# Another searched order of the same jobs: a one-core transformer layer with windowed attention and a gated MLP

## Chip, core and metric

The kernel runs on one core of one Trainium2 chip. The metric is the device time of one launch in microseconds (us). Before the change the median of three runs is 244.9 us (244.74 to 245.12).

## What is computed

One layer on 2048 tokens of width 448: an attention part with 16 heads of 28, in which a query sees 8 keys at distances 0, 2, ... 14, and then a gated MLP (width 896 twice) whose gate mixes all tokens by a 2048 x 2048 matrix.

```python
def _A_ref(x, wqkv, wo):
    qkv = (x @ wqkv).reshape(B, S, 3, H, Dh).transpose(2, 0, 3, 1, 4)
    ...
    logits = jnp.einsum('bhsd,bhswd->bhsw', q, kg) * scale
    logits = jnp.where(mask[None, None, :, :], logits, -1000000000.0)
    o = jnp.einsum('bhsw,bhswd->bhsd', _softmax(logits), vg)
    return o.transpose(0, 2, 1, 3).reshape(B, S, D) @ wo

def _B_ref(x, w_in, w_sp, b_sp, w_out):
    z = _gelu(jnp.einsum('bsd,df->bsf', x, w_in))
    z1, z2 = z[..., :Fh], _layernorm(z[..., Fh:])
    g = jnp.einsum('ts,bsf->btf', w_sp, z2) + b_sp[None, :, None]
    return jnp.einsum('bsf,fd->bsd', z1 * g, w_out)
...
h = x + _A_ref(_layernorm(x), A_wqkv, A_wo)
h2 = h + _B_ref(_layernorm(h), B_w_in, B_w_sp, B_b_sp, B_w_out)
```

## The kernel before

The program is written as some 890 **jobs**. A job is a short run of instructions on one engine: PE (matmul), ACT, DVE, POOL, or SP, which issues the DMAs. The engines run their own lists, in the order in which the jobs stand in the table `ORDER`, and each instruction waits on semaphores for what it needs. Nothing is reordered when the kernel runs: an instruction that waits holds all that stands behind it on its engine. Further tables belong to that order: `BANKS` gives each matmul group its PSUM banks, `ON` puts a copy on another engine than its default, and `MODE` tells how a matmul product over 448 rows (three full chunks of 128 and a rest of 64) is split into two jobs a and b: FH (full chunks, then the rest), HF (rest first), or AB, in which each chunk is taken as two halves of 64 rows that run on the two halves of the array, so that a and b each do one half. Number 885 in `ORDER` is a small matmul without use, `warm` (L1077), that keeps PE busy while it has nothing to do.

The stages, as the names in this document have them (the lines are those of the profile):

- **Loads** (L519): x in five pieces and more, named by their first tile of 128 tokens (x0, x1, x2 with x3, x4 with x5, x6 with x7, x8 with three more, x12 with three more), the q,k weights wq in five pieces (wq0, wq1, wq2 of 128 rows, wq3 and wq4 of 64), wv and wo in three pieces each, w_in in eight.
- **Layernorm of x** by tile: statistics st (L620) and mv (L622) on DVE, the power of -1/2 on POOL (L611), the normalisation n (L631) into a ring xn, and a copy nd (L504) that doubles the last 64 columns, on POOL or DVE. Tiles 0 to 3 are transposed on PE (L661) and copied to xhT by xe; tiles 4 to 15 by a transposing DMA xT (L518).
- **q,k**: wp copies wq into a padded wqk (L504); qk0 and qk1 (128 tokens each, L704), qk2 (256), qk3, qk4, qk5 (512 each, L461, in four groups), copied to qkT by qe.
- **Attention** in 17 blocks b of up to 128 keys: the value product v (L461, two blocks at once), logits lg (L809, two halves), exponentials ex (ACT, L818), a mask multiplication mk on DVE (L824), the block product o (L833), the division (rc, om: L841, L844), a doubling copy od, a transposing DMA oT, and a copy oc that interleaves even and odd tokens.
- **Projection** y (two tiles at once, L461), the add h on DVE (L774), the second layernorm, and a transposing DMA hT of two tiles.
- **MLP**: z2 and z1 (L461) with gelu on ACT, statistics and normalisation of z2, the gate products g (L987, L1008) with w_sp, which is loaded by 32 transposing DMAs wlo and whi, the gate's add and multiplication on DVE (L968, L971), and the output product wo (L1035, L1056), add and store.

All DMAs are issued by SP, one after the other. A transposing DMA keeps SP for about 1.3 us:

```python
def dma_T(name, dst, src, reads, writes, key):
    return load(name, dst, src, writes, 1.27, (TLAT, 0.56), key=key, transpose=True, reads=reads)
```

What a product waits for follows from what it reads. The value product of blocks b and b + 1 reads the x tiles that these blocks cover, so v4 needs the tiles 3, 4 and 5; qk5 needs the tiles 12 to 15:

```python
product("v%d" % b, key, f, r_wv + xh_res(lo, hi), D, tk, [o_jobs.get(b + i - NV) for i in range(nb)])
```

The order is fixed by one function that reads the tables:

```python
def order(self):
    for t, b in zip(self.tickets, BANKS):
        t.b = b
    return [self.jobs[i] for i in ORDER]
```

Of the kernel before, what the change touches and what calls it, by code (L numbers as in the profile page):

```python
# [9 lines left out]
FH = 896  # L10
# [9 lines left out]
NPT = 4  # L20
TLAT = 0.67
MODE = {'qk2_0': 'AB', 'qk2_1': 'AB', 'qk2_2': 'AB', 'qk2_3': 'FH', 'qk3_0': 'AB', 'qk3_1': 'AB', 'qk3_2': 'AB',
# [8 lines left out]
ORDER = [6, 26, 42, 27, 43, 29, 0, 885, 30, 885, 1, 31, 885, 885, 7, 885, 885, 28, 12, 885, 32, 885, 2, 52, 885, 134,  # L31
# [40 lines left out]
BANKS = [2, 1, 2, 1, 6, 4, 2, 6, 4, 0, 4, 0, 4, 0, 6, 4, 0, 0, 2, 4, 4, 4, 2, 4, 6, 3, 6, 6, 6, 6, 0, 4, 6, 7, 2, 0,  # L72
# [4 lines left out]
KEY = dict(x=-10.145, xs=0.685, qk=-3.702, qkg=-1.064, v=-1.761, ve=-6.148, qe=-3.15, lg=-1.488, ex=5.497,  # L77
           mk=-3.215, o=2.696, om=0.603, oT=-1.054, hh=0.0, y=-5.759, h=0.564, ln2=4.478, hT=19.942, z2=74.834,
           z2s=0.028, zr=2.556, zrs=0.21, z1=34.42, z1s=2.041, g=84.462, gs=0.172, wo=1.509, wl=-9.273,
           wls=4.361, wp=-9.955)  # L80
WINB = 2
ON = {'xe3_0': 'dve', 'nd0_4': 'dve', 'nd0_5': 'dve', 'nd0_7': 'dve', 'nd0_8': 'dve', 'nd0_10': 'dve', 'nd0_13':
         'dve', 'nd0_14': 'dve', 'qe3_1': 'dve', 'qe4_1': 'dve', 'qe4_2': 'dve', 've0': 'dve', 'od0': 'dve', 'od2':
         'dve', 'oc2': 'act', 'oc3': 'act', 'od5': 'dve', 'oc5': 'dve', 'nd1_2': 'dve', 've6': 'dve', 'od6': 'dve',
         'oc6': 'act', 'od7': 'dve', 've8': 'dve', 'oc8': 'act', 'od9': 'dve', 'oc9': 'act', 'oc9b': 'act', 'nd1_6':
         'dve', 'oc10': 'dve', 'oc11': 'act', 'nd1_8': 'dve', 've12': 'dve', 'od12': 'dve', 'nd1_11': 'dve', 'oc14':
         'dve', 'nd1_12': 'dve', 'od16': 'dve', 'nd1_15': 'dve', 'z2c10': 'dve'}
RAW2 = [0, 1, 2, 1, 1, 1, 1, 2, 1, 2, 1, 0, 0, 1, 0, 0]
XEH = {0: 2}
WLH = [4, 4, 8, 9, 18, 1, 4, 12, 24, 4, 14, 34, 6, 22, 21, 26]  # L90
# [1044 lines left out]
```

## Time and profile before

| | |
|---|---|
| median of the runs | 244.9 us |
| the profiled execution's own time | 247.0 us |
| its span, first to last instruction | 245.3 us |
| mean granted TensorE clock | 0.993 |
| weight loads of PE | busy 122.3 us, beside the matmuls |
| shares of the chain that ended last | PE 80%, DMA 8%, DVE 7%, ACT 1% |
| median from issue to landing: x in pieces of 224 KB | 3.4 us |
| the same: wq in pieces of 224 KB | 4.5 us |
| the same: transposes OTs, hnT, wsp_hi | 2.9, 3.8, 4.2 us |

Sizes of the loads: x 112 KB a tile; wq 224 KB for each of the three large pieces and 56 KB for each of the two small ones; wv and wo 336 KB and twice 56 KB each. The chain that ended last is found from the end of the execution backwards: at each step what released an instruction, or the one before it on its engine. The engines' busy times overlap. The rows of the profile stand in the prediction, where they are used.

### The profile page before, as it was taken

Reading aid. Unit: us, or ns where it says so; the run is one execution under the profiler, and the core shown is the slowest. Engines: PE = TensorE matmul, PEld = TensorE weight load, DVE = VectorE, ACT = ScalarE, POOL = GpSimd, SP = SyncE. Lnnn points to the kernel's source line nnn. Section 1 sums busy time; section 2 is a strip of 40 time slices with the busy share of each in tenths; the row PEclk is TensorE's granted clock in tenths of the full one; section 3 lists DMA queues with packets and bytes.
Section 4 is the critical chain, followed back from the end, with each engine's and each line's share of the span. In section 5 each row is a group of like instructions: output and inputs, shape, how many; then the busy total and the mean of one; then the engine's idle time right before and its main releaser. Section 6 shows DMA issues by size and latency. Waiting matters only on the chain.

```text
span 245.3 us, 5632 instructions
## 1 busy us (share of the span) xinstructions
PE 237.2 (97%) x2422; PEld 122.3 (50%) x2422; DVE 147.6 (60%) x334; ACT 91.1 (37%) x109; POOL 42.5 (17%) x98
## 2 busy tenths in 40 slices
PE   7997999999999989999999999999999999999995
PEld 4763544554555534444555555555554444444453
DVE  5998685998999897899913030604217350060584
ACT  2485748968899956659711000000000000000000
POOL 6625022030533317052311000000000000000000
PEclk9997999999999999999999999999999999999999
DMA  6953527989688889957999700000000020000022
GB/s 175 294 157 70 129 61 110 189 174 186 128 107 112 88 146 225 253 59 134 166 178 181 141 3 0 3 0 3 0 3 0 0 92 24 0 3 0 3 90 97
DMA packets 66233, 23.20 MB, mean 95 GB/s; under 512 B 58656, under 2 KB 65952, under 8 KB 66208
## 3 DMA queue, kind: packets, MB, share of 16 engines
q1 hardware_dynamic: 66208, 22.83, 48.5%
q8 instruction: 19, 0.31, 0.5%
q14 instruction: 6, 0.05, 0.1%
HBM read 6.72 MB, written 1.84 MB: 35 GB/s over the span
## 4 chain that ended last, share of the span: by engine, by line
PE 80%; DMA 8%; DVE 7%; ACT 1%; SPq 1%; issue 1%; POOL 0%
PE psum L987 37%; PE psum L461 27%; PE psum L1035 7%; DMA hnT<-xn 4%; PE psum L1008 3%; PE psum L809 2%; PE psum L833 2%; PE psum L1056 2%; DMA wq<-in_A_wqkv_dram 2%; DVE st L620 2%; DMA xhT<-xn 2%; DVE E L824 1%; DVE xn L631 1%; DMA OTs<-otm 1%; DVE x_tm L774 1%; SPq L519 1%
## 5 line engine op out<-in xcount | busy, mean ns | idle before, releaser
L968 DVE TENSOR_TENSOR ub<-psum,bb 128x512 bf16<-128x512 f32 x28 | 18.1, 686 | 64.4 <-PE psum L987 64.4
L987 PE MATMUL psum<-wsp_hi,z2p 64*128 64x512 bf16 x384 | 42.2, 376 | 0.0
L818 ACT ACTIVATE E<-psum 128x960 bf16<-128x960 f32 (+2 forms) x34 | 31.5, 976 | 6.3 <-PE psum L809 6.3
L987 PEld LDWEIGHTS psum<-wsp_hi,z2p 64*128 64x128 bf16 x384 | 19.7, 94 | 21.9 <-DVE srg L1016 0.4
L987 PE MATMUL psum<-wsp_lb,z2p 64*128 64x512 bf16 x224 | 26.9, 376 | 0.0
L987 PE MATMUL psum<-wsp_la,z2p 64*128 64x512 bf16 x224 | 26.5, 376 | 0.0
L461 PE MATMUL psum<-w_in,hnT 64*128 64x448 bf16 (+1 forms) x206 | 24.6, 350 | 0.2 <-issue 0.2
L461 PE MATMUL psum<-hnT,w_in 64*128 64x512 bf16 (+1 forms) x166 | 23.7, 377 | 1.1 <-DMA hnT<-xn 0.9
L461 PE MATMUL psum<-xhT,wqk 64*128 64x512 bf16 (+3 forms) x206 | 24.4, 355 | 0.1
L898 DVE BATCH_NORM_STATS2 st<-z2p 128x6 f32<-128x448 bf16 x32 | 19.0, 610 | 8.0 <-ACT z2p L894 6.0
L824 DVE TENSOR_TENSOR E<-E,maskb 128x1920 bf16<-128x1920 bf16 (+2 forms) x17 | 19.8, 1183 | 2.9 <-ACT E L818 2.9
L620 DVE BATCH_NORM_STATS2 st<-x_tm 128x6 f32<-128x448 bf16 x32 | 18.8, 613 | 1.4 <-DMA x_tm<-in_A_x_dram 1.3
L987 PEld LDWEIGHTS psum<-wsp_lb,z2p 64*128 64x128 bf16 x224 | 12.8, 94 | 11.4
L987 PEld LDWEIGHTS psum<-wsp_la,z2p 64*128 64x128 bf16 x224 | 12.8, 94 | 11.4
L611 POOL TENSOR_TENSOR rs<-rs,negh 128x2 f32<-128x2 f32 (+2 forms) x23 | 17.4, 758 | 3.0 <-DVE rs L610 1.1
L936 ACT ACTIVATE z1p<-psum 128x1024 bf16<-128x1024 f32 x14 | 14.1, 1023 | 10.0 <-PE psum L461 10.0
L1035 PE MATMUL psum<-w_out,z1p 128*128 128x448 bf16 x84 | 16.4, 353 | 0.0
L461 PEld LDWEIGHTS psum<-w_in,hnT 64*128 64x128 bf16 (+1 forms) x206 | 10.9, 94 | 10.8 <-issue 1.0
L461 PE MATMUL psum<-wv,xhT 64*128 64x448 bf16 (+1 forms) x92 | 14.9, 367 | 1.4 <-DMA xhT<-xn 1.4
L504 ACT ACTIVATE qkT<-psum 128x1024 bf16<-128x1024 f32 (+1 forms) x17 | 13.3, 824 | 6.9 <-PE psum L461 4.2
L461 PEld LDWEIGHTS psum<-hnT,w_in 64*128 64x128 bf16 (+1 forms) x166 | 9.6, 95 | 12.4 <-DVE x_tm L774 1.4
L461 PEld LDWEIGHTS psum<-xhT,wqk 64*128 64x128 bf16 (+1 forms) x206 | 10.0, 95 | 9.8 <-issue 0.8
(68 smaller groups left out, 254.6 us busy)
## 6 DMA issues: line engine op xcount, KB each, us to landing
w_in<-in_B_w_in_dram SPq DMA_DIRECT2D x8, 224.0 KB, 3.7
out_dram<-srg SPq DMA_DIRECT2D x16, 112.0 KB, 1.7
x_tm<-in_A_x_dram SPq DMA_DIRECT2D x2, 448.0 KB, 5.2
w_out<-in_B_w_out_dram SPq DMA_DIRECT2D x1, 784.0 KB, 5.1
wq<-in_A_wqkv_dram SPq DMA_DIRECT2D x3, 224.0 KB, 4.5
x_tm<-in_A_x_dram SPq DMA_DIRECT2D x3, 224.0 KB, 3.4
bb<-in_B_b_sp_dram SPq DMA_DIRECT2D x1, 512.0 KB, 4.8
wv<-in_A_wqkv_dram SPq DMA_DIRECT2D x1, 336.0 KB, 4.8
```

What stands on the lines that cost most here:

```text
L461: ins = e.matmul(o, w, x, start=k not in seen, stop=last, **kw)
L504: j = pl.job(name, eng, key, [(lambda e: e.activation(o(), i(), AF.Copy) if eng == "act" else e.tensor_copy(o(), i()), list(reads), list(w ...
L611: power = (lambda e: e.tensor_tensor(R, A, negh[:, 0:1].to_broadcast([128, n]), ALU.pow), [rr, r_negh], r_rs[k][m:m + n])
L620: [(lambda e: e.bn_stats(st[:, m, :], src), [rsrc], [r_st[k][m]])], dve_t(D))
L818: return e.activation(o, i, AF.Exp, scale=SCALE)
L824: return e.tensor_tensor(a, a, maskb[:, mi:mi + 1, pad:pad + nq].to_broadcast([NK, NHEAD, nq]), ALU.mult)
L898: [(lambda e, m=m, k=k: e.bn_stats(st3[:, m, k, :], z2p[:, m, D * k:D * (k + 1)]), [r_z2[m]], [r_st[2][m]])], dve_t(D))
L936: return e.activation(o, i, AF.Gelu_apprx_tanh)
L968: [(lambda e: e.tensor_tensor(ub[:, s, :], psv(tk, k), bb[:, 512 * tc:512 * tc + 512], ALU.add), [r_bb], [r_ub[s]])], dve_t(512), use=[tk] ...
L987: ins = e.matmul(psv(tk, k), z2p[h, s, 128 * fc:128 * fc + 128], wsp(s, tc)[h], start=n == 0 and s == 0, stop=n == len(lots) - 1 and s == ...
L1008: ins = e.matmul(psv(tk), z2p[:, s, 128 * fc:128 * fc + 128], wsp(s, tc), start=(s == 0), stop=(s == NB - 1))
L1035: ins = e.matmul(psv(tk, k, D), z1p[h, fc, 128 * (m + k):128 * (m + k) + 128], w_out[h, fc, :], start=fc == 0 and (which == 0 or not half) ...
```

## The change

The jobs are the same but for the number of `warm` matmuls and for the splits in `MODE`; their order (`ORDER`), banks (`BANKS`), engines (`ON`) and splits are another solution of the same search. The tables' first differing rows:

```diff
-ORDER = [6, 26, 42, 27, 43, 29, 0, 885, 30, 885, 1, 31, 885, 885, 7, 885, 885, 28, 12, 885, 32, 885, 2, 52, 885, 134,
...
+ORDER = [6, 29, 33, 26, 134, 0, 34, 7, 885, 27, 885, 1, 885, 885, 31, 2, 885, 885, 885, 52, 11, 885, 42, 885, 32, 3,
...
-ON = {'xe3_0': 'dve', 'nd0_4': 'dve', 'nd0_5': 'dve', 'nd0_7': 'dve', 'nd0_8': 'dve', 'nd0_10': 'dve', 'nd0_13':
...
+ON = {'xe0_1': 'act', 'xe1_0': 'dve', 'xe2_0': 'dve', 'xe3_0': 'dve', 'nd0_6': 'dve', 'nd0_8': 'dve', 'nd0_10': 'dve',
+         'nd0_12': 'dve', 'nd0_13': 'dve', 'nd0_14': 'dve', 'nd0_15': 'dve', 'wp1': 'act', 'wp2': 'act', 'qe2_3':
...
```

The file is one line longer, so each line of the program stands one lower.

In `MODE` 16 products had FH or HF before and 15 have it now. In `ON` the weight copies wp1 and wp2 and the second half of x's tile 0 go from DVE to ACT, the evacuations of tiles 1 and 2 from ACT to DVE, nd0_4 and nd0_5 from DVE to POOL; of the q,k copies DVE has five and not three, of the V copies two and not four, of the z2 copies two and not one.

**SP's queue at the start.** The names x_tm, wq and wo are the loads of x, of the q,k weights and of the output weights; a form 128x448 is one tile of x, 128x2x448 two. Before (the third row is x2 and x6, the last one x4):

```order
L519 DMA x_tm<-in_A_x_dram 128x448 x2
L519 DMA wq<-in_A_wqkv_dram 128x896
L519 DMA x_tm<-in_A_x_dram 128x2x448 x2
L519 DMA wq<-in_A_wqkv_dram 128x896
L519 DMA wq<-in_A_wqkv_dram 64x448
L519 DMA wq<-in_A_wqkv_dram 128x896
L519 DMA wq<-in_A_wqkv_dram 64x448
L519 DMA wo<-in_A_wo_dram 64x448
L519 DMA wv<-in_A_wqkv_dram 64x448
L519 DMA x_tm<-in_A_x_dram 128x2x448
```

Now (the pairs of tiles are x2, x4 and x6, in this order):

```order
L520 DMA x_tm<-in_A_x_dram 128x448 x2
L520 DMA x_tm<-in_A_x_dram 128x2x448
L520 DMA wq<-in_A_wqkv_dram 128x896 x2
L520 DMA x_tm<-in_A_x_dram 128x2x448
L520 DMA wq<-in_A_wqkv_dram 128x896
L520 DMA wo<-in_A_wo_dram 128x3x448
L520 DMA wq<-in_A_wqkv_dram 64x448 x2
L520 DMA x_tm<-in_A_x_dram 128x2x448
```

x2 and x4 moved ahead; x6 moved back, behind the last pieces of wq, which themselves stand behind the large piece of wo.

**PE around the first product that needs a tile transposed by DMA (v4).** The names V and E are the values and the exponentials, qkT holds q and k; the first 448 wide rows are v0 before and v2 now, the last row is v4. Before:

```order
L461 MATMUL psum<-wv,xhT 128x448 [waits sem_pe]
L461 MATMUL psum<-wv,xhT 128x448 x5
L809 MATMUL psum<-qkT 128x120 [waits sem_act]
L809 MATMUL psum<-qkT 128x120 x7
L461 MATMUL psum<-wv,xhT 128x448 [waits sem_q20,sem_q18,sem_act]
```

Now:

```order
L462 MATMUL psum<-wv,xhT 128x448 [waits sem_pe]
L462 MATMUL psum<-wv,xhT 128x448 x5
L834 MATMUL psum<-V_81,E 128x29 [waits sem_act,sem_dve]
L834 MATMUL psum<-V_81,E 128x29 x15
L462 MATMUL psum<-wv,xhT 128x448 [waits sem_q19,sem_q18,sem_act]
```

The block product o0 (V, E) moved ahead of v4, the logits beside v0 moved elsewhere, and tile 5, whose landing the first semaphore of the last row tells, is the second transpose that SP issues (q19) and not the third (q20).

**SP's queue around the transpose of h's tiles 6 and 7 (hT6, hnT).** OTs rows are the transposes oT of attention blocks, wsp_lb those of w_sp. Before:

```order
L518 DMA_TRANSPOSE OTs<-otm 128x4x128 [waits sem_pool,sem_act,sem_dve]
L518 DMA_TRANSPOSE OTs<-otm 128x4x128 [waits sem_dve]
L518 DMA_TRANSPOSE wsp_lb<-in_B_w_sp_dram 128x1024 [waits sem_pe]
L518 DMA_TRANSPOSE hnT<-xn 128x8x128 [waits sem_pool]
L518 DMA_TRANSPOSE OTs<-otm 128x4x128 [waits sem_pool,sem_dve]
```

Now:

```order
L519 DMA_TRANSPOSE OTs<-otm 128x4x128 [waits sem_pool,sem_dve]
L519 DMA_TRANSPOSE OTs<-otm 128x4x128 [waits sem_pool]
L519 DMA_TRANSPOSE hnT<-xn 128x8x128 [waits sem_pool,sem_dve]
L519 DMA_TRANSPOSE wsp_lb<-in_B_w_sp_dram 128x1024 [waits sem_pe]
```

The transpose of w_sp moved from ahead of hT6 to behind it, and the second OTs row (oT12) waits for a copy on POOL and no longer for one on DVE.

On PE, further, the first job of qk5 moved from place 79 of its list to place 68, right behind qk4; and the first half of z2_1 moved to between the last logits ahead of the add h4 and the one behind it.

More of the change, by code (lines that the diff above doesn't have):

```diff
@@ L22 @@
 MODE = {'qk2_0': 'AB', 'qk2_1': 'AB', 'qk2_2': 'AB', 'qk2_3': 'FH', 'qk3_0': 'AB', 'qk3_1': 'AB', 'qk3_2': 'AB',
[8 rows of a table removed]
-ORDER = [6, 26, 42, 27, 43, 29, 0, 885, 30, 885, 1, 31, 885, 885, 7, 885, 885, 28, 12, 885, 32, 885, 2, 52, 885, 134,
[40 rows of a table removed]
-BANKS = [2, 1, 2, 1, 6, 4, 2, 6, 4, 0, 4, 0, 4, 0, 6, 4, 0, 0, 2, 4, 4, 4, 2, 4, 6, 3, 6, 6, 6, 6, 0, 4, 6, 7, 2, 0,
[4 rows of a table removed]
[8 rows of a table added]
+ORDER = [6, 29, 33, 26, 134, 0, 34, 7, 885, 27, 885, 1, 885, 885, 31, 2, 885, 885, 885, 52, 11, 885, 42, 885, 32, 3,
[40 rows of a table added]
+BANKS = [2, 1, 1, 6, 2, 4, 2, 0, 6, 6, 0, 2, 2, 0, 0, 4, 6, 2, 4, 6, 6, 0, 2, 4, 0, 4, 4, 4, 7, 0, 6, 6, 6, 6, 0, 2,
[4 rows of a table added]
 KEY = dict(x=-10.145, xs=0.685, qk=-3.702, qkg=-1.064, v=-1.761, ve=-6.148, qe=-3.15, lg=-1.488, ex=5.497,
@@ L81 @@
 WINB = 2
-ON = {'xe3_0': 'dve', 'nd0_4': 'dve', 'nd0_5': 'dve', 'nd0_7': 'dve', 'nd0_8': 'dve', 'nd0_10': 'dve', 'nd0_13':
[L83 to L87, printed above, removed]
+ON = {'xe0_1': 'act', 'xe1_0': 'dve', 'xe2_0': 'dve', 'xe3_0': 'dve', 'nd0_6': 'dve', 'nd0_8': 'dve', 'nd0_10': 'dve',
+         'nd0_12': 'dve', 'nd0_13': 'dve', 'nd0_14': 'dve', 'nd0_15': 'dve', 'wp1': 'act', 'wp2': 'act', 'qe2_3':
+         'dve', 'qe3_1': 'dve', 'qe4_1': 'dve', 'qe4_2': 'dve', 'qe5_0': 'dve', 'od0': 'dve', 'oc1': 'dve', 'nd1_0':
+         'dve', 'nd1_1': 'dve', 've2': 'dve', 'od2': 'dve', 'oc2': 'dve', 'oc3': 'act', 'od4': 'dve', 'oc4': 'act',
+         'oc5': 'dve', 'nd1_2': 'dve', 'nd1_3': 'dve', 've6': 'dve', 'oc6': 'act', 'od8': 'dve', 'oc8': 'act', 'oc8b':
+         'dve', 'od9': 'dve', 'od10': 'dve', 'oc11': 'act', 'nd1_8': 'dve', 'nd1_9': 'dve', 'oc12': 'dve', 'oc13':
+         'act', 'oc14': 'dve', 'oc15': 'act', 'nd1_15': 'dve', 'z2c5': 'dve', 'z2c9': 'dve'}
 RAW2 = [0, 1, 2, 1, 1, 1, 1, 2, 1, 2, 1, 0, 0, 1, 0, 0]
```

102 rows, old and new, of tables (BANKS, MODE, ORDER) are left out of this document.

## The prediction, made before the changed kernel had run

> **What bounds the kernel now.** I read the page's busy line, then stretches of the span by engine, then the chain that ended last, then PE, SP and the durations of single shapes.
>
> ```profile
> PE 237.2 (97%) x2422; PEld 122.3 (50%) x2422; DVE 147.6 (60%) x334; ACT 91.1 (37%) x109; POOL 42.5 (17%) x98
> 13.00:20.35 7.35, 7.16 (x116) 4.55 (x104) 7.35 (x25) 6.41 (x10) 2.05 (x4) 1.00 0.51 127
> 20.35:21.65 1.30, 0.00 (x0) 0.02 (x1) 1.30 (x4) 1.30 (x2) 1.22 (x3) 1.00 0.33 35
> 21.65:25.40 3.75, 3.74 (x28) 1.40 (x30) 2.04 (x9) 1.29 (x3) 0.99 (x4) 0.54 0.36 74
> 25.40:65.00 39.60, 39.42 (x562) 19.82 (x558) 33.92 (x61) 29.60 (x34) 8.74 (x16) 1.00 0.73 133
> 65.00:75.00 10.00, 9.37 (x147) 4.86 (x144) 9.30 (x20) 9.12 (x14) 3.64 (x8) 1.00 0.82 136
> 75.00:90.00 15.00, 14.05 (x181) 7.41 (x180) 14.25 (x31) 14.05 (x16) 3.55 (x8) 1.00 0.91 114
> 123.60:245.00 121.40, 119.00 (x991) 59.77 (x985) 39.41 (x80) 1.94 (x2) 0.93 (x2) 1.00 0.19 40
> ```
>
> From the second row on stand, for each stretch, its length, then busy time of PE, weight loads, DVE, ACT and POOL, then the granted clock. PE is the bound: from 25.4 us on it hardly rests, and from 123.6 us nothing else matters (the gate products of L987, the ninth row below, begin). A new order cannot remove matmul work, so it can win only what PE loses: 1.30 us of rest before 21.65 us, the 3.75 us behind it at a clock of 0.54, and the rests between 65 and 90 us. It can lose by making new ones. DVE and ACT, over 90% busy from 65 to 90 us, are where new ones threaten.
>
> ```profile
> 3.16 4.68 DMA wq<-in_A_wqkv_dram
> 11.10 1.04 DVE st L620 x2
> 12.35 0.28 DVE xn L631
> 12.63 0.60 DVE xhT L504
> 17.16 0.09 DVE xn L504
> 17.35 4.17 DMA xhT<-xn
> 28.23 0.90 PE psum L833 x32
> 84.11 5.21 DMA hnT<-xn
> 123.64 5.18 PE psum L987 x48
> 21.66 2.62 PE L461 MATMUL psum<-wv,xhT 128*128 128x448 bf16 x8 [1.36 <-DMA xhT<-xn]
> 67.52 0.39 PE L809 MATMUL psum<-qkT 28*128 28x120 bf16 x8 [0.47 <-DVE x_tm L774]
> 68.07 0.93 PE L461 MATMUL psum<-w_in,hnT 64*128 64x448 bf16 x8 [0.16 <-issue]
> 89.45 0.71 PE L461 MATMUL psum<-hnT,w_in 64*128 64x512 bf16 x3 [0.94 <-DMA hnT<-xn]
> ```
>
> The first nine rows are the chain (start, length), the last four PE's timeline with the rest before each row. The chain is loads, then DVE without a pause, then one transposing DMA of x's tile 5 that lands at 21.52 us, for which v4 (the value product of blocks 4 and 5) waits 1.36 us. Later PE rests 0.47 + 0.16 us at the add h4 and 0.94 us at the transpose hT6. These four rests and the low clock are the whole stock: 1.36 + 0.47 + 0.16 + 0.94 + 3.75 × (1 − 0.54) = 1.73, together 4.66 us.
>
> **The change part by part.** *The start.* On SP's queue the pair x2 comes third, x4 sixth (it was twelfth), and x6 eleventh (it was fifth). The sixth load was issued at 3.16 us and landed at 7.84; x4 in that place, with the same bytes ahead, lands near 7.9, and DVE's two statistics of it (11.10 us before) can start three us sooner. The weights do not gain: wo (336 KB) now stands ahead of wq's last pieces, so 1792 KB go before their end instead of 1456.
>
> ```profile
> 5.80 0.62 DVE L620 BATCH_NORM_STATS2 st<-x_tm 128x6 f32<-128x448 bf16 x1
> 5.00:10.00 5.00, 4.51 (x61) 3.62 (x59) 4.44 (x16) 0.98 (x2) 3.56 (x9) 1.00 0.92 273
> L504 DVE COPY wqk<-wq 128x896 bf16<-128x896 bf16 x3 | 1.2, 391 | 0.8 <-DMA wq<-in_A_wqkv_dram 0.8
> ```
>
> At 273 GB/s 336 KB are 1.2 us: the last copy, wp3, begins no sooner than 10.5 us. That costs nothing, since DVE comes to it only near 11.0 (from 5.0 on, by the list below, four statistics, four normalisations, three evacuations, one weight copy and five small ones: 2.1 + 1.2 + 1.8 + 0.4 + 0.5); without that cover PE would start 0.5 us later. wp1 and wp2 leave DVE (0.39 us each) for ACT, which idles there.
>
> *v4.* x2's statistics began at 5.80 us; with x2 one load earlier I take 5.0. From there DVE's list ahead of tile 5's normalisation is now six statistics at 0.53, six normalisations at 0.30, three evacuations at 0.60, two weight copies together 0.6 and some eight small ones at 0.1: 3.2 + 1.8 + 1.8 + 0.6 + 0.8 = 8.2, so it ends near 13.2.
>
> ```profile
> L504 POOL COPY xn<-xn 128x64 bf16<-128x64 bf16 x15 | 4.7, 317 | 10.8 <-DVE xn L631 10.8
> DMA to landing us min/median/max: 2.4/2.5/4.2
> ```
>
> POOL's copy adds about 0.4, so the transpose that SP issued at 17.35 us (DVE's own copy stood behind a mask multiplication until 17.25) goes out near 14, second instead of third of its kind. With 2.5 to 4.2 us from issue to landing (the second row is that of the transposes into xhT) it is there by 16.5 to 18.2. On DVE, x6's statistics are queued ahead of tile 4's normalisation: each us x6 lands after 11.2 delays both transposes and the first mask, which has 0.9 us of slack (by the same list DVE ends it near 19.7, and PE comes to o0, which needs it, near 20.6); v4 has three. On PE the block product o0 (half of 0.90 us in the chain's row below) now goes ahead of v4. What is late next there is ACT.
>
> ```profile
> 7.62 3.87 PE L704 MATMUL psum<-xhT,wqk 128*128 128x128 bf16 x64
> 10.64 2.07 ACT L504 ACTIVATE qkT<-psum 128x512 bf16<-128x512 f32 x4 [2.77 <-PE psum L704]
> 11.42 0.34 PE L661 MATMUL psum<-ident,xn 128*128 128x128 bf16 x3
> 11.87 0.34 PE L661 MATMUL psum<-ident,xn 128*128 128x128 bf16 x3
> L818 ACT ACTIVATE E<-psum 128x1024 bf16<-128x1024 f32 x4 | 4.0, 1021 | 0.2 <-PE psum L809 0.2
> L504 ACT ACTIVATE V<-psum 128x896 bf16<-128x896 f32 x4 | 3.7, 917 | 3.1 <-PE psum L461 3.1
> ```
>
> The second of the first q,k products ended at 11.5 us; two tile transposes (0.45 us apart) now go ahead of it: 12.4. Then seven copies, overlapped at about 0.5 (four took 2.07 us), three exponentials and a V copy (four at 0.95): 12.4 + 3.6 + 3.8 = 19.8, plus 1.0 for the exponential that frees v4's banks and 0.2 of waits: 21.0. PE would thus start v4 at 21.0 with o0 done, against 21.66 without: 0.66 + 0.45 = **1.1 us** of the 1.36. Bounds: 0 (ACT a full us later) to 1.4. The low clock follows the rest, so with no rest over 0.5 us it goes: **1.73** (bounds 0 and 1.73).
>
> *h4.* z2_1's first half (eight of the 64x448 products, 0.93 us in its row) now stands between y4 and the matmul that waits for h4's bank: of 0.63 us I take **0.5** (0 to 0.63).
>
> *hT6.* On SP a transpose of w_sp (wlo12) is no longer ahead of hT6, and the oT12 before it waits for POOL's copy, not for a DVE copy behind two masks.
>
> ```profile
> 82.77 1.29 SPq L518 DMA_TRANSPOSE wsp_lb<-in_B_w_sp_dram  x1
> hnT<-xn SPq DMA_TRANSPOSE x8, 3.8
> ```
>
> hT6 goes out at least 1.29 us sooner against PE's progress; that covers 0.94, more so if it lands in the median 3.8 and not 5.21: **0.9** (0 to 0.94).
>
> *New rests.* All other waits move too.
>
> ```profile
> L504 DVE CAST qkT<-psum 128x1024 bf16<-128x1024 f32 x3 | 3.7, 1225 | 3.2 <-PE psum L461 3.2
> L504 DVE CAST z2p<-psum 128x896 bf16<-128x896 f32 x1 | 1.1, 1092 | 0.2 <-PE psum L461 0.2
> L504 DVE CAST V<-psum 128x896 bf16<-128x896 f32 x4 | 4.3, 1080 | 0.1
> ```
>
> DVE gains two evacuations of x (0.6 each, one of them for a half one of 0.3), one q,k copy of 0.6 and one of 1.2 and one z2 copy of 1.1; it loses two V copies (1.1 each) and wp1, wp2 (0.8): 1.2 − 0.3 + 1.8 + 1.1 − 2.2 − 0.8 = +0.8 us net, and small copies of xn, otm and OT change between POOL, DVE and ACT; with 14% free from 25.4 to 65 us it is hidden; between 65 and 90 it is not. I take **−0.7** for waits of 0.1 to 0.3 us on ACT and DVE (bounds 0 and −3: the 0.63 and 0.95 us that PE rests between 65 and 90 us, doubled).
>
> The sum: 1.1 + 1.73 + 0.5 + 0.9 − 0.7 = 3.5 us. The profiled execution took 247.0 us, of which 245.3 is its span; the span falls to 241.8, and the median of 244.9 to **241.4 us**.
>
> **A rule against this sum.** The clock was 0.54 in the stretch behind a rest of 1.36 us. The Trainium skill (TensorE: Matmul & The Clock Gate, What's actually happening) says the gate closes after at least one idle window of about 3.4 us and that the window runs free of the kernel. By that rule 1.36 us would not close it. The trace disagrees as far as it goes: 3.75 × 0.46 × 2 = 3.45 us at half clock follow the only long rest of that part.
>
> **The rivals.** *First, the low clock comes without the gap:* partial use of PE before 20 us, not the rest, sets it. For it: PE's matmuls up to 13 us are short ones. Against: the clock is 1.00 all through that time. The gain is 3.5 − 1.73 = 1.8: 243.1 us. It is also what the rule of the Trainium skill above would leave. *Second, the gaps come back elsewhere* between 65 and 90 us, where ACT and DVE are full: the new rests reach −3, gain 1.2, 243.7 us. *Third, slower: the last q,k products (qk5, tokens from 1536 on) wait for x's last tile.*
>
> ```profile
> 37.46 1.27 SPq L518 DMA_TRANSPOSE xhT<-xn  x1
> 49.55 2.43 PE L461 MATMUL psum<-xhT,wqk 64*128 64x512 bf16 x14
> 43.36 0.81 PE L461 MATMUL psum<-xhT,wqk 64*128 64x512 bf16 x6
> ```
>
> That tile's transpose left at 37.46 us, near 40 it landed, and its first user came at 49.55. In the new order qk5_2 follows qk4_3 (done at 44.17 before) at once, so PE is there near 41.8 if it leads by 2.4. SP issues the transpose at 36.5 to 38.8 (a w_sp transpose of 1.3 us is now ahead, tile 14 up to 2.2 sooner); it lands 2.5 to 4.2 us later, 39.0 to 43.0. A wait of up to 1.2 us is hidden nowhere: lg6_1, v8 and o4 stand behind it on PE, and ACT's exponentials wait for those. From a landing at 43.6 on, a wait of 1.8 and a second low-clock stretch of 1.73 eat the 3.5, and with DVE's chain late as well it becomes 246.5 us. For it: cover falls from 9.6 us to about one. Against: at the median of 2.5 us it is there in time even from the latest issue. *Fourth, the change does not do what it says:* the weights arrive later, not sooner (above); ACT's start then slips by the uncovered part, up to 1.2 us, and with the clock kept low nothing remains: 244.9 us.
>
> **How the numbers follow.** The forecast has 0.55 (239.9 to 242.6), the first rival 0.10, the second 0.11, the third 0.19, the fourth 0.05. Faster by over 0.2% (0.5 us, what a measurement of this kernel can tell) are the first three: 0.75, less 0.01 at the edge, 0.74; slower 0.19 plus half of the fourth, 0.21; within, 0.05. The range reaches to 239.9 (all bounds at their best: 4.66 plus 0.3) and to 245.8, within the third rival, leaving some 0.17 out.
>
> **What would show it.** Right: no rest over 0.5 us before v4, started at 20.5 to 21.5 us with a tile transpose landed by 18.5; a clock of 1.00 from 13 us on; no wait on hnT near 85 us; PE's steady part after z2 and z1 starting near 120, not 123.6. Wrong: a PE rest on xhT near 42 us, rests on ACT over 0.5 us between 60 and 80, or a low-clock stretch anywhere before 120.

## The result, and the profile after

The changed kernel takes **243.18 us** (median of 4 runs, 242.87 to 243.51), the kernel before 244.90 (244.74 to 245.12): ratio 0.9933, 95% interval 0.9908 to 0.9957. It is faster, by 1.7 us, where 3.5 were forecast. Yet the span of the profiled execution fell from 245.3 to 241.8 us, exactly the forecast. Both are right: every execution takes about 1.7 us more than its span, so the 244.90 of the runs belong to a span of 243.2, and the profiled execution of before was 2.1 us longer than an ordinary one.

The busy line of the page of after:

```profile
PE 235.9 (98%) x2431; PEld 116.3 (48%) x2431; DVE 149.3 (62%) x336; ACT 92.0 (38%) x109; POOL 40.0 (17%) x96
```

PE is still the bound, and its share of the span rose from 97 to 98%. The stretches of after, the same as those that the prediction shows of before (length, then busy time of PE, weight loads, DVE, ACT, POOL, then the granted clock):

```profile
13.00:20.35 7.35, 7.35 (x123) 4.50 (x117) 6.89 (x19) 6.86 (x11) 2.75 (x7) 1.00 0.56 123
20.35:21.65 1.30, 1.20 (x25) 0.63 (x22) 1.19 (x4) 1.30 (x3) 0.54 (x2) 1.00 0.00 0
21.65:25.40 3.75, 3.73 (x33) 1.56 (x34) 3.75 (x12) 2.61 (x3) 0.00 (x0) 1.00 0.37 60
25.40:65.00 39.60, 39.03 (x566) 19.30 (x564) 34.79 (x72) 30.60 (x35) 7.50 (x14) 1.00 0.71 135
65.00:75.00 10.00, 9.67 (x142) 5.03 (x138) 9.86 (x22) 9.23 (x14) 4.47 (x8) 1.00 0.90 141
75.00:90.00 15.00, 14.74 (x172) 7.38 (x168) 14.79 (x30) 12.22 (x15) 3.98 (x9) 1.00 0.91 154
```

Length less PE's busy time is what PE rests. Before, the six stretches had 0.19 + 1.30 + 0.01 + 0.18 + 0.63 + 0.95 = 3.26 us of it; now it is 0 + 0.10 + 0.02 + 0.57 + 0.33 + 0.26 = 1.28. So 1.98 us of rest are gone. The clock of the third stretch went from 0.54 to 1.00, which the prediction's formula makes 1.73 us more.

PE's timeline at the places of the three old rests (v4, h4, hT6) and at the two largest new ones, with the rest before a row in brackets:

```profile
21.67 1.61 PE L462 MATMUL psum<-wv,xhT 128*128 128x448 bf16 x8
31.91 0.56 PE L834 MATMUL psum<-V,E 128*128 128x29 bf16 x16 [0.40 <-DVE E L825]
65.38 0.93 PE L462 MATMUL psum<-w_in,hnT 64*128 64x448 bf16 x8 [0.33 <-ACT E L819]
66.24 0.42 PE L810 MATMUL psum<-qkT 28*128 28x120 bf16 x16
78.45 0.37 PE L462 MATMUL psum<-w_in,hnT 64*128 64x448 bf16 x2 [0.26 <-DMA hnT<-xn]
84.08 1.03 PE L462 MATMUL psum<-hnT,w_in 64*128 64x512 bf16 x8
```

v4 (first row) starts without a rest, but no sooner than before, at 21.67 us. The logits behind h4 (fourth row) and the first product with hT6 (last row) no longer wait. New are 0.40 us at the block product o1, for mask mk1, 0.33 for an exponential ahead of z2_1, and 0.26 for the transpose hT4.

### The profile page after: what moved, and what is told of

It reads as the page before. It is cut to its first block, busy times and chain, and to the rows that moved or that the text cites. A ratio compares the mean times of both kernels' runs of the same rounds, so it can differ in the third digit from the quotient of the medians.

```text
span 241.8 us, 5654 instructions
## 1 busy us (share of the span) xinstructions
PE 235.9 (98%) x2431; PEld 116.3 (48%) x2431; DVE 149.3 (62%) x336; ACT 92.0 (38%) x109; POOL 40.0 (17%) x96
## 4 chain that ended last, share of the span: by engine, by line
PE 88%; DVE 6%; ACT 2%; DMA 2%; issue 0%
PE psum L988 37%; PE psum L462 31%; PE psum L1036 7%; PE psum L1009 3%; PE psum L1078 3%; PE psum L1057 2%; DMA hnT<-xn 2%; PE psum L834 2%; PE psum L810 2%; DVE E L825 2%; ACT E L819 2%; PE psum L705 1%; DVE x_tm L775 1%; DVE st L621 1%; ACT V L505 1%; DVE xn L632 1%
## 5 line engine op out<-in xcount | busy, mean ns | idle before, releaser
L988 PEld LDWEIGHTS psum<-wsp_hi,z2p 64*128 64x128 bf16 x384 | 18.5, 94 | 23.0 <-issue 0.4
L988 PE MATMUL psum<-wsp_lb,z2p 64*128 64x512 bf16 x224 | 26.4, 376 | 0.0
L1017 DVE TENSOR_TENSOR srg<-psum,x_tm 128x448 bf16<-128x448 f32 (+1 forms) x17 | 9.5, 591 | 14.0 <-PE psum L1036 12.0
L988 PEld LDWEIGHTS psum<-wsp_lb,z2p 64*128 64x128 bf16 x224 | 10.8, 94 | 13.4
L988 PEld LDWEIGHTS psum<-wsp_la,z2p 64*128 64x128 bf16 x224 | 10.8, 94 | 13.1 <-DVE ub L969 0.2
L462 PE MATMUL psum<-wv,xhT 64*128 64x448 bf16 (+1 forms) x86 | 14.2, 354 | 0.3 <-ACT V L505 0.2
L505 ACT ACTIVATE qkT<-psum 128x1024 bf16<-128x1024 f32 (+1 forms) x15 | 11.7, 828 | 7.2 <-PE psum L462 4.2
```

The source lines that it names most:

```text
L462: ins = e.matmul(o, w, x, start=k not in seen, stop=last, **kw)
L505: j = pl.job(name, eng, key, [(lambda e: e.activation(o(), i(), AF.Copy) if eng == "act" else e.tensor_copy(o(), i()), list(reads), list(w ...
L988: ins = e.matmul(psv(tk, k), z2p[h, s, 128 * fc:128 * fc + 128], wsp(s, tc)[h], start=n == 0 and s == 0, stop=n == len(lots) - 1 and s == ...
L1017: [(lambda e: e.tensor_tensor(srg[:, s, c0:c1], psv(tk, k, c1 - c0), x_tm[:, m, c0:c1], ALU.add), [r_x[m]], r_srg[2 * s + (c0 > 0):2 * s + ...
```

## The experiments

The question is why the span kept the forecast and the median did not. **Theory A**: the low clock was in that one execution; the order's own gain is 1.8 us. **Theory B**: it is in every execution of the kernel before, and after loses half of its gain elsewhere. Every kernel below is compared with the kernel before on the same chip. "Under 0.998" counts the executions whose mean granted clock is lower than that.

```
kernel                            executions  under 0.998  median us  ratio to before (95% interval)
before, all four series               98          19         245.18 at full clock, 246.84 below
after, three series                   16           0         243.2    0.9933, 0.9926, 0.9929
before, xT5 earlier                   12           0         244.03   0.9956 (0.9935 to 0.9976)
before, wlo12 behind hT6               9           1         243.89   0.9944 (0.9917 to 0.9971)
before, both, first series             6           0         242.61   0.9882 (0.9834 to 0.9931)
before, both, with after beside it     6           0         242.87   0.9917 (0.9888 to 0.9945)
before, xT5 later                     12           7         247.23   1.0074 (1.0035 to 1.0113)
before, xT5 later, rest filled        10           0         247.64   1.0077 (1.0045 to 1.0108)
after, six fillers fewer              12           0         243.54   0.9927 (0.9896 to 0.9958)
after, xT15 one place later           12           0         244.44   0.9962 (0.9931 to 0.9993)
after, v6 and hT4 moved               12           0         244.33   0.9964 (0.9940 to 0.9988)
```

**The kernel before, and the changed one, again.** No edit.

> The kernel before, unchanged, to see the clock and the span of executions other than the one that was profiled first. Theory A (the low clock is an accident of single executions: the window of the clock runs free, and only where the 1.36 us of rest before v4 falls wholly into one window does the clock halve): most executions show a mean clock of 1.00 and a span near 245.3 - 1.7 - 0.4 = 243.2 us, a few show 0.993 and 245.3. Theory B (the low clock is in every execution of this order): all show 0.993 and 245.3 us, and the 244.9 us of the runs are then explained otherwise.

> The changed kernel, unchanged, on the same chip as the one before. Theory A: clock 1.00 and spans of 241.2 to 241.8 us in all executions, 1.7 us (0.993) faster than the kernel before. Theory B: as low clock is gone for good, 3.5 us between the spans, the rest of it lost around the span.

Theory A holds. In this series before was executed 38 times; 5 executions showed 0.993 with spans of 244.7 to 245.2 us, the other 33 showed 0.999 or 1.00 with 242.1 to 244.2. Over all series it is 19 of 98, and they take 246.84 us in the median against 245.18, 1.66 us apart, about the term of 1.73. None of them took under 246.38 us, so the runs behind the 244.9 (at most 245.12) had no low clock, though theirs is not on record. The changed kernel has none in 16. The profiled execution of before in this series fell among the five, and shows a rest ahead of v4 again:

```profile
22.16 2.89 PE L461 MATMUL psum<-wv,xhT 128*128 128x448 bf16 x8 [1.91 <-DMA xhT<-xn]
```

**One local edit for each old rest.** Job names; a row with + is where it goes, with - where it was. First, the transpose of tile 5:

```diff
 DVE   st0_10
+DVE   nd0_5
 DVE   mk0
-DVE   nd0_5
 SP    xT4
+SP    xT5
 SP    xT7
-SP    xT5
```

> Before, with one local edit: the copy nd0_5 ahead of the mask multiplication mk0 on DVE, and the transpose xT5 ahead of xT7 on SP. It goes out at 16.1 instead of 17.35 us and lands by 18.6 to 20.3, so v4 waits for the exponential ex2_0 (20.1) alone and the rest of 1.36 us shrinks to 0.1. Theory A: the median falls by the rest alone, 1.1 to 1.3 us (ratio 0.995), and the clock is 1.00 as it mostly was. Theory B: by the rest and the low clock, 2.8 to 3.0 us (0.988). A third: nothing (1.000), because ACT, which had caught up in the rest, is late next and PE rests at the following jobs instead.

The median fell by 1.3 us, theory A's number, with full clock in all 12. In its profile, v4's rest is gone and the rest for hT6 is still there (the view ends at 90 us and cuts the second row):

```profile
19.90 1.61 PE L461 MATMUL psum<-wv,xhT 128*128 128x448 bf16 x8
87.44 2.87 PE L461 MATMUL psum<-hnT,w_in 64*128 64x512 bf16 x13 [1.05 <-DMA hnT<-xn]
```

Second, hT6:

```diff
 SP    oT12
-SP    wlo12
 SP    hT6
+SP    wlo12
```

> Before, with one move on SP: the transpose wlo12 of w_sp behind the transpose hT6 instead of ahead of it. hT6 goes out at 82.8 instead of 84.1 us and lands by 86.6 to 88.0, before PE comes to z1_3 at 88.5: the rest of 0.94 us goes and the median falls by 0.9 us (ratio 0.996). The rival: the rests that follow (0.6 us between 90 and 100) take it up, and the gain is under 0.3 us.

The median fell by 1.4 us (0.7 to 2.0 by the interval), so hT6's rest is not taken up by those behind it. PE did not rest at all in the stretch in question:

```profile
75.00:90.00 15.00, 15.00 (x148) 7.21 (x145) 14.28 (x34) 11.88 (x13) 4.49 (x10) 1.00 0.70 112
```

Both together:

> Before with both local edits together (xT5 and its copy earlier; wlo12 behind hT6). If the two rests add up: 1.3 + 1.4 = 2.7 us off 245.3, 242.6, which is below the changed kernel's 243.2 with two moved rows. If ACT and DVE, late behind PE, take the second gain back: 243.5 to 243.9, no better than one edit alone.

They add up: 2.7 us. Then the same kernel again, beside the changed one on one chip:

> The kernel before with its two local edits (xT5 and nd0_5 earlier, wlo12 behind hT6) again, now on one chip with the changed kernel: 242.6 us as on the other chip, 0.4 to 0.8 us below the changed kernel. If the difference was the chips': no difference.

> The changed kernel, unchanged, on the same chip: 243.2 us, no execution with a mean clock under 0.999 (so far 0 of 10).

242.87 against 243.26 there (2.5 us under the kernel before), and 242.61 in the series ahead of it against 243.2 of the changed kernel: three moved rows of the old order are at least as good as the new order, and by the medians 0.4 to 0.6 us better, though the intervals of the two ratios overlap. This is the fastest kernel of the study. It keeps before's wait for h4:

```profile
PE psum L809 <- DVE x_tm L774: 0.4, 1, 0.4
```

**Does the rest bring the low clock?** xT5 one place later:

```diff
-SP    xT5
 SP    xT6
+SP    xT5
 SP    xT9
```

> Before with xT5 moved back by one more transpose (behind xT6): it lands at 21.2 to 22.9 us, so PE rests up to 2.5 us before v4. Theory A (the rest within one window of the clock decides): a rest of 2.5 us leaves at least 1.25 us in one window whatever its phase, so most executions have the low clock (mean 0.993), against 5 of 38 with the rest of 1.4 to 1.7: time 245.3 + 1.1 + 1.7 = 248.1. If the low clock is a chance that has nothing to do with the rest: again one in eight, median 246.4.

7 of 12 executions have the low clock instead of 19 of 98, and the time rises to 247.23; "most" holds narrowly, and the 248.1 was too high. PE's timeline of the profiled one, at v4:

```profile
22.97 2.89 PE L461 MATMUL psum<-wv,xhT 128*128 128x448 bf16 x8 [3.04 <-DMA xhT<-xn]
```

and its stretches, whose last column but two is the granted clock:

```profile
20.00:22.97 2.97, 0.00 (x1) 0.03 (x2) 2.43 (x7) 1.49 (x2) 1.87 (x5) 0.83 0.21 19
22.97:25.80 2.83, 2.83 (x10) 0.83 (x11) 0.94 (x5) 0.00 (x0) 0.24 (x1) 0.50 0.47 96
25.80:28.80 3.00, 3.00 (x30) 1.24 (x30) 1.09 (x1) 2.64 (x3) 0.00 (x0) 0.50 0.70 163
```

A rest of 3.04 us is followed by nearly 6 us at half clock, with PE busy throughout.

The clock records of the traces tell more than these views. They change in steps of 3.413 us, counted from each trace's first record. The low clock begins at 21.96, 21.95 and 21.96 us in the three profiles that have it (before twice, and this kernel) and lasts 3.41, 3.41 and 6.83 us. Here it begins 1 us ahead of v4, while PE still rests. In the step just ahead of it PE rested 1.36, 1.70 and 2.04 us. In this kernel the first low step holds 1.00 us of rest, and a second one follows. The nine other profiles with such records have no low clock, and no step with more than 1.11 us of rest between matmuls. These traces fit a limit between 1.11 and 1.36 us of rest within one step, with the low clock in the step behind it; that the rest within a step counts, and not the whole rest, they do not separate. Of a rest of 3.04 us one step holds at least half, 1.5, wherever the steps fall, so the five executions at full clock must have rested less if this limit holds for them.

The same kernel, with the rest filled:

```diff
 PE    lg3_1
+PE    warm x24 (bank 4 instead of 0 for all warm matmuls)
 PE    v4a
```

> The kernel before with xT5 late as in the run with the lengthened rest, but 24 filler matmuls (0.11 us each, 2.6 us) ahead of v4, so that PE waits as long without resting. Theory A (PE's rest brings the low clock): no execution has a mean clock under 0.999, where 7 of 12 had it without the fillers, and the time is that of its executions at full clock, 246.0 to 246.7 us, up to a us more where xT5 lands early and the fillers are still in front of v4. If the low clock follows the late transposes or the work behind them: again about half of the executions, median 247.2 or more.

No execution of 10 has the low clock. PE's timeline:

```profile
20.24 2.79 PE L1077 MATMUL psum<-warm 128*128 128x256 bf16 x24
22.87 1.60 PE L461 MATMUL psum<-wv,xhT 128*128 128x448 bf16 x8
```

v4 starts as late as with the rest of 3.04 us, and runs in 1.60 us instead of 2.89. It is the rest of PE, not the late transpose, that the clock follows. The fillers have a price: 247.64 us are 1.5 more than the 246.16 (median) of the five executions at full clock without them, and in the profile xT5 had landed at 21.92 us, 0.95 before v4 started.

**The start of the changed kernel.**

```diff
 PE    xT1
-PE    warm x6
 PE    xT0
```

> The changed kernel without the six filler matmuls between the transposes of tile 1 and tile 0. In the changed order n0_0 is done at 7.29 us and xT1 at 7.38, yet xT0 ends at 8.79, because the six fillers (1.06 us) stand ahead of it; PE has no rest from there on. If the start's term fell short because of fillers that cover no wait: the first q,k products and v4 come up to 1.0 us sooner and the time falls by 0.5 to 1.0 us (to 242.2 to 242.7). If ACT's or DVE's chain (the weight copies wp1 to wp3, then the exponentials) sets the start: no gain, within 0.3 us of 243.2, and PE rests at qk1F2 and qk0H instead; with over 1.3 us of rest in one window the clock could also halve, 1.7 us more.

No gain: 0.9927 against 0.9926 and 0.9929. The fillers cost nothing that the median shows: without them PE waits for DVE in their place, and v4 starts at 20.48 us, hardly sooner than in two profiles with them (20.61 and 20.75):

```profile
7.01 0.34 PE L662 MATMUL psum<-ident,xn 128*128 128x128 bf16 x3 [0.33 <-DVE xn L632]
20.48 1.61 PE L462 MATMUL psum<-wv,xhT 128*128 128x448 bf16 x8
```

**The third rival, priced.** xT15 one place later in the changed kernel:

```diff
-SP    xT15
 SP    oT3
+SP    xT15
```

> The changed kernel with the transpose of x's last tile (xT15) one place later on SP, behind oT3. In the profiled execution it landed 0.18 us before PE came to qk5_2. This prices the third rival of the prediction: xT15 lands near 43.5 to 45 us, PE rests 1 to 2.3 us before qk5_2 and the time is 1 to 2.3 us over 243.2; with a low clock behind it up to 4 us. If the rest is made up later (ACT and DVE late anyway, PE not the bound at 42 to 66 us): under 0.3 us.

1.2 us more than the changed kernel (244.44 against 243.2), no low clock in 12. PE rests before qk5_2 for what the transpose is late (the row names another releaser; by the landings, xT15 came at 43.58 us and PE started at 43.72):

```profile
43.72 1.04 PE L462 MATMUL psum<-xhT,wqk 64*128 64x512 bf16 x8 [1.11 <-ACT qkT L505]
```

**The new rests.**

```diff
+PE    v6a
 PE    o1
-PE    v6a
+SP    hT4
 SP    oT10
-SP    hT4
```

> The changed kernel with its two largest new rests taken away: v6's first product ahead of o1, which waits 0.4 us for the mask multiplication mk1, and the transpose hT4 ahead of oT10 on SP, for which PE waits 0.3 us near 78 us. If the new rests cost what the waits show (the term taken at 0.7 us in the prediction): 0.5 to 0.7 us off 243.2. If PE only waits for ACT or DVE a little later: under 0.2 us.

It became 1.1 us slower. In this order hT4 also stands ahead of POOL's doubling copy nd of h's tile 5 and reads these 64 columns before they are written; the amount of work is the same. The two rests went and others came:

```profile
33.98 1.90 PE L462 MATMUL psum<-xhT,wqk 64*128 64x512 bf16 x16 [0.21 <-DVE otm L845]
80.67 0.56 PE L834 MATMUL psum<-V,E 128*128 128x29 bf16 x16 [0.57 <-DVE otm L845]
```

PE waits for the next divisions instead. Which of the two moves cost the rest of the 1.1 us was not separated.

## Why the prediction was right, and where it was wrong

**What bounds it, and the stock of losses.** Right: PE is the bound in both, and what was won came out of its rests.

**The term that failed is the low clock, "it goes: 1.73".** The mechanism was right in the profiled pair: the clock of that stretch went from 0.54 to 1.00 as the rest went, and the span fell by 3.5 us. That it fell by just the forecast is in part luck: two later profiles of the changed kernel have 240.9 and 241.0 us, not 241.8. But the sum was then taken from a median in which the loss was not: "the span falls to 241.8, and the median of 244.9 to 241.4". The rows to see it by stood in the prediction's own text: the profiled execution took 247.0 us, 2.1 over the median and 1.9 over the slowest of the three runs (245.12), about the size of the one term that an accident of the clock can bring. Without the term the sum is 1.1 + 0.5 + 0.9 − 0.7 = 1.8 us; the three series show 1.7, 2.2 and 2.1.

**The first rival's number, 243.1, is the measured one, its mechanism is not.** It had the low clock come without the gap and stay; in fact it is mostly absent on both sides. The rule beside it, that the gate closes after at least one idle window of about 3.4 us (the Trainium skill, TensorE: Matmul & The Clock Gate, What's actually happening), does not agree with these runs: rests of 1.36, 1.91 and 3.04 us, all shorter, were followed by half clock. That the window runs free of the kernel, which the same section says, fits the clock records: their first step comes at 4.9 us in the three profiles with a low clock and between 5.5 and 8.0 in the nine without. That this phase decides which 19 executions of 98 have it is not shown: the rest ahead of v4 differs between executions too (1.36, 1.91 and none in three profiles), and only profiles tell either. Against this rival the prediction set a clock of 1.00 all through the start; for the first 5 us that does not hold (last section).

**v4 and the start, 1.1.** Right in size, by another way than worked out. xT5 was issued at 15.26 us, not near 14, and landed at 17.69, within 16.5 to 18.2; PE's rest from 20.35 to 21.65 us fell from 1.30 to 0.10 us with o0 done ahead of v4. v4's start was forecast at 21.0: it is 21.67 in the first profile, and 20.61 and 20.75 in two later ones of the same kernel. DVE ended mk0 at 20.30 instead of 19.7.

**h4, 0.5.** The wait for h4 (0.47 + 0.16 us) is gone; 0.33 us for an exponential stands at the same place. Net 0.3.

**hT6, 0.9.** Right: no wait for it in after, and its move alone is worth 1.4 us (0.7 to 2.0).

**New rests, −0.7.** The size was near, the place wrong. 25.4 to 65 us was to hide what is added, "with 14% free"; PE's rest there rose from 0.18 to 0.57 us, while between 65 and 90 us it fell from 1.58 to 0.59 in all. An engine's free share does not say that the one mask PE needs is ready.

**The other rivals.** The second (gaps come back at 65 to 90 us) did not occur. The third was as near as can be: xT15 landed at 42.48 us, within 39.0 to 43.0, and qk5_2 started at 42.62. In two later profiles it landed at 41.53 and 41.63 and qk5_2 started at 41.67 and 41.76. Some 0.14 us also lie between landing and start where PE did rest for a tile (21.52 and 21.66 before v4, 43.58 and 43.72 in the run above), so no slack was left. Its price was too high, though: a landing 1.1 us later costs 1.2 us and brings no low clock, against the 246.5 us that took in such a clock and a late DVE. The fourth (no effect) fell; the late weights were hidden as argued, wp3 ended at 11.96 us and its first user came at 12.72. One sign was badly chosen: gate products now begin at 115.43 us among the last of z1, so the start of their steady part tells nothing. And the chances of the first three add up to 0.76, not 0.75.

## What to carry to other kernels

Before a loss in a profile is put into a sum, compare the profiled execution's own time with the runs: what only that execution has can't be won from the median. Look for a lower granted clock first, since it came here behind a rest of TensorE of 1.4 to 3 us, and in a share of the executions only; filling the rest with matmuls kept the clock up, but only an earlier transfer won the time. And where few rests are left, each with one late job, move those jobs one at a time: three moved rows were worth as much here as a whole new order.

## What the runs showed of the hardware that was not expected

**The start runs at half clock for a time that differs between executions.** The small fillers on PE near 7 us, in the first and in the second profile of the changed kernel (the second view ends at 7 us and cuts off the sixth filler):

```profile
7.29 1.14 PE L1078 MATMUL psum<-warm 128*128 128x256 bf16 x6
```

```profile
6.53 0.72 PE L1078 MATMUL psum<-warm 128*128 128x256 bf16 x5
20.61 1.61 PE L462 MATMUL psum<-wv,xhT 128*128 128x448 bf16 x8
```

By the ends of single fillers they take 0.21 us until about 8 us in the first and until 5.6 us in the second, 0.11 behind that; before had this step at 4.9 us. The granted clock of the views reads 1.00 all the while; the traces' clock records begin only at this step, at 7.95, 5.55 and 4.89 us. The spans are 241.8 and 240.9 us. So v4 starts about a microsecond apart in two profiles of one kernel (21.67 and 20.61). The Trainium skill says of cold matmuls at a kernel's start that their count differs from run to run with the free window (TensorE: Matmul & The Clock Gate, What's actually happening), and these rows agree.

**A transposing DMA lands about 1.6 us later when 16 KB of instructions are read while it is under way.** From the DMA packets and semaphores of the traces (us):

```
execution                       tile  issued  landed  took  read of 16 KB
before, first profile           xT5   17.35   21.52   4.17  19.26
before, second profile          xT5   17.78   22.03   4.25  19.16
before, wlo12 behind hT6        xT5   16.93   19.41   2.48  19.33 (it was landing)
the same                        xT6   18.24   22.43   4.19  19.33
before, xT5 earlier             xT5   15.81   18.23   2.42  none
the same                        xT7   17.04   21.07   4.02  19.01
after                           xT15  38.49   42.48   3.98  39.50
after, xT15 one place later     xT15  41.07   43.58   2.51  none
```

The delay stays with the moment, not with the tile: moved out of it, xT5 and xT15 land in 2.4 to 2.5 us, and xT7, moved in, takes 4.0. In the third row the read comes 0.5 us later against the issue than in the first, xT5 escapes, and PE does not rest before v4 in that execution. So v4's rest is not a constant of the order either: 1.36 and 1.91 us in two profiles and none in the third. The reads seem to be TensorE's: about 250 of its matmuls and weight loads start between one read and the next, on average, so an order also sets what they collide with. That the read causes the delay was not tried by moving a read alone.
